# A new order for one core's 111 large transfers and the work between them, in a kernel with a branch near its end

## The chip, the cores and the metric

The kernel runs on one core of a Trainium2 chip. The metric is the device time of one execution in microseconds (us): 263.57 us is the median of three runs before the change (263.34 to 264.36).

## The reference

Four batches of 12,544 queries, keys and values of width 128, with 49 agent vectors per batch. Agents attend to keys and values, queries attend to agents, and a three-way maxout feed-forward network of width 768 follows.

```python
def sm(a, b):
    s = scale * (a @ b.transpose(0, 2, 1))
    s = s - s.max(-1, keepdims=True)
    e = np.exp(s)
    return e / (e.sum(-1, keepdims=True) + 1e-09)
agent_v = sm(agents, k) @ v
x = (sm(q, agents) @ agent_v).reshape(B * S, D)
h = np.maximum(np.maximum(x @ w1, x @ w2), x @ w3)
return (h @ w_out).astype(np.float32)
```

Inputs and output are float32 and live in HBM: some 78.7 MB are read and 25.7 MB written.

## The kernel before

**Keys and values.** Each batch is cut into 14 chunks of 896 rows; two chunks come in one load of 896 KB (`kl`, `vl`, line 274 issues them). A chunk of keys is cast to bf16 on POOL (`kc`), transposed on PE (`kt`), copied out of PSUM by DVE (`ke`), scored against the agents on PE (`ks`) and exponentiated on ACT (`kx`). A chunk of values is cast (`vc`, on ACT for batch 0, on POOL after that), and PE accumulates the products (`kv`).

**The batch's matrices.** When the last chunk of batch b is in, DVE normalises (`nr`, lines 352 and 353), PE multiplies by differences of the weights (`pu`, `pv`), ACT and DVE find for each agent and hidden unit which of the three maxout branches wins (`vs`, `tm`, `rd`, lines 369 to 391), PE counts the units whose winner isn't the same for all agents (`ps`), DVE gives them slots (`sl`, lines 409 to 412), and PE, ACT and DVE fill a matrix G of the batch (`px`, `py`, `gx`, `gy`), with which the network's work on a query becomes small.

**Queries.** 49 groups of 1,024 queries, two to a load of 1,024 KB (`ql`, line 476), group 48 with a half load of its own. A group is cast on POOL (`qc`, line 488), transposed (`qt`) and copied out by ACT (`qe`, line 494), scored (`sc`), exponentiated (`ex`, line 507), summed (`su`, `re`), multiplied by G (`u`, `v`), passed through the maxout (`a` on ACT, `x` on DVE, line 530), multiplied out into two PSUM banks (`li`, `p`) and scaled by DVE into an output slot (`ov`, line 546). Two groups share an output slot and one store of 1,024 KB (`st`, line 481); the last three stores are of 512 KB.

**The branch.** After the fourth batch's `sl`, DVE reduces the slot counts to one number in `most` (`fullest`, lines 416 and 417). Every engine loads that number (line 244) and branches on it (line 245): over the limit of 64 the general path would run, else the `Else` block goes on with the rest of the order. With these inputs it is the `Else` block. Nothing behind the branch is issued on an engine before that engine has taken it.

**What sets the order.** All this is one list of names, `ORDER`, in which `|` is the branch and a number behind a slash the buffer slot that the step's new tile takes; the program is emitted in exactly that order, and each engine runs its own part of it in order. SP issues all loads and stores and nothing else. There are 10 load slots (`LD`), 7 output slots (`OS`), 8 PSUM banks (`M`) and a few bf16 buffers of each kind. A load waits until the casts from its slot's old tile are done, and a scaling into an output slot until the store from it has landed, seven stores back. Transfers carry one of eight completion semaphores in turn: in the built program every transfer from the eighth on waits for the one eight places before it, so that at most eight are under way.

## Time and profile before

| | us |
|---|---|
| median of three runs | 263.57 |
| the profiled execution | 263.26 |
| its span, first to last instruction | 261.5 |
| what lies around the span | 1.76 |
| PE busy | 204.4 |
| DVE busy | 163.7 |
| ACT busy | 143.8 |
| POOL busy | 146.4 |

A row of the page's second part cuts the span into 40 slices of 6.54 us; its digits are tenths, its GB/s what the core's 16 DMA queues moved. SP is never counted as busy: its rows in a timeline are the issues of transfers. "Landing" is the time from a transfer's issue to the last of its 16 parts.

### The profile page before, as it was taken

How to read it: one execution, taken by the hardware profiler on the slowest of the kernel's cores; microseconds unless marked ns; L12 is line 12 of the kernel's file. 1: busy time of each engine (PE TensorE's matmuls, PEld its weight loads, DVE VectorE, ACT ScalarE, POOL GpSimd, SP SyncE). 2: the span in 40 equal slices, each digit the busy share in tenths (PEclk: the TensorE clock that was granted, in tenths of full speed). 3: DMA queues.
4: the chain of work that ended last, by engine and by line, in shares of the span. 5: the costliest groups of instructions: out<-in, count | busy, mean ns of one | idle time of the engine just before them, and what ended most of it. 6: DMA issues, size and time to landing. Idle time of an engine off the chain costs nothing.

```text
span 261.5 us, 7474 instructions
## 1 busy us (share of the span) xinstructions
PE 204.4 (78%) x3049; PEld 159.5 (61%) x3049; DVE 163.7 (63%) x337; ACT 143.8 (55%) x236; POOL 146.4 (56%) x164
## 2 busy tenths in 40 slices
PE   0775868699999995999877798867889645999950
PEld 0654657478778774787765576654666434777730
DVE  5352314748678779696657886641667833788980
ACT  1453555356677772637745665615457641899710
POOL 2423355997888869576765775475845561354000
PEclk9995595779999999799999999977999995999996
DMA  7999999999999999999999999999999976999995
GB/s 259 412 404 410 420 417 414 420 418 418 418 420 422 414 420 418 427 416 418 422 427 417 424 426 420 423 422 419 427 420 422 418 305 231 373 421 421 415 427 222
DMA packets 17639, 105.01 MB, mean 402 GB/s; under 512 B 1783, under 2 KB 3771, under 8 KB 11579
## 3 DMA queue, kind: packets, MB, share of 16 engines
q1 hardware_dynamic: 17392, 104.34, 97.1%
q8 instruction: 26, 0.43, 0.7%
q14 instruction: 18, 0.15, 0.2%
q10 hardware_dynamic: 203, 0.10, 0.1%
HBM read 78.74 MB, written 25.69 MB: 399 GB/s over the span
## 4 chain that ended last, share of the span: by engine, by line
DMA 72%; PE 19%; issue 2%; ACT 2%; DVE 1%; POOL 1%; DVEq 0%; SPq 0%; POOLq 0%; ACTq 0%
DMA LD<-in_q_dram 28%; DMA LD<-in_v_dram 23%; DMA LD<-in_k_dram 15%; PE psum L258 14%; DMA LD<-in_moe_w_out_dram 5%; PE psum L289 4%; ACT QT L494 1%; POOL QB L488 1%; DVE OS L546 1%; POOL KB L284 0%; ACT EK L304 0%; DVE R L530 0%; DVE KT L295 0%; ACT EQ L507 0%; DVEq L741 0%
## 5 line engine op out<-in xcount | busy, mean ns | idle before, releaser
L488 POOL CAST QB<-LD 128x1024 bf16<-128x1024 f32 x49 | 50.2, 1048 | 44.7 <-DMA LD<-in_q_dram 25.0
L546 DVE TENSOR_TENSOR OS<-psum,RC 128x512 f32<-128x512 f32 x98 | 63.4, 684 | 18.1 <-PE psum L258 16.0
L284 POOL CAST KB<-LD 128x896 bf16<-128x896 f32 x56 | 51.8, 951 | 39.9 <-DMA LD<-in_k_dram 34.0
L494 ACT ACTIVATE QT<-psum 128x1024 bf16<-128x1024 bf16 x49 | 50.3, 1026 | 33.0 <-PE psum L289 31.0
L295 DVE COPY KT<-psum 128x896 bf16<-128x896 bf16 x56 | 34.0, 614 | 32.5 <-PE psum L289 32.0
L284 POOL CAST VB<-LD 128x896 bf16<-128x896 f32 x42 | 38.6, 946 | 5.5 <-DMA LD<-in_v_dram 4.8
L258 PE MATMUL psum<-G,EQ 128*128 128x256 bf16 x196 | 38.7, 279 | 1.5 <-issue 1.5
L507 ACT ACTIVATE EQ<-psum 128x512 bf16<-128x512 f32 x49 | 29.1, 601 | 18.8 <-PE psum L258 18.4
L289 PE MATMUL psum<-ident,KB 128*128 128x128 bf16 x392 | 34.5, 242 | 6.3 <-POOL KB L284 5.8
L258 PE MATMUL psum<-G,R 128*128 128x256 bf16 x196 | 38.7, 280 | 0.7 <-DVE R L530 0.7
L289 PE MATMUL psum<-ident,QB 128*128 128x128 bf16 x392 | 31.8, 227 | 8.9 <-POOL QB L488 4.5
L289 PEld LDWEIGHTS <-QB 128*128 128x128 bf16 x392 | 26.4, 102 | 17.4 <-POOL QB L488 6.5
L530 DVE TENSOR_TENSOR R<-psum,AS 128x512 bf16<-128x512 f32 x49 | 33.1, 677 | 6.3 <-ACT AS L527 4.8
L527 ACT ACTIVATE AS<-psum 128x512 bf16<-128x512 f32 x49 | 29.2, 601 | 14.0 <-PE psum L258 8.4
L289 PEld LDWEIGHTS <-KB 128*128 128x128 bf16 x392 | 27.7, 109 | 11.6 <-POOL KB L284 8.1
L258 PE MATMUL psum<-QT,agT 128*128 128x512 bf16 (+1 forms) x104 | 30.9, 386 | 4.9 <-ACT QT L494 4.6
L304 ACT ACTIVATE EK<-psum 128x343 bf16<-128x343 f32 x56 | 24.7, 459 | 15.5 <-PE psum L258 14.4
L258 PEld LDWEIGHTS <-EQ 128*128 128x128 bf16 x392 | 26.8, 98 | 10.2 <-ACT EQ L507 2.8
L258 PE MATMUL psum<-EQ,G 128*128 128x512 bf16 (+1 forms) x104 | 31.8, 373 | 0.0
L258 PEld LDWEIGHTS <-ones 128*128 128x128 bf16 x417 | 19.1, 100 | 14.4 <-issue 11.8
L258 PE MATMUL psum<-EK,ones 128*128 128x49 bf16 x392 | 20.1, 190 | 5.9 <-ACT EK L304 5.9
L258 PEld LDWEIGHTS <-KT 128*128 128x128 bf16 x392 | 16.5, 102 | 9.6 <-DVE KT L295 6.2
(81 smaller groups left out, 201.5 us busy)
## 6 DMA issues: line engine op xcount, KB each, us to landing
LD<-in_k_dram SPq DMA_DIRECT2D x28, 896.0 KB, 18.2
LD<-in_v_dram SPq DMA_DIRECT2D x28, 896.0 KB, 18.1
LD<-in_q_dram SPq DMA_DIRECT2D x24, 1024.0 KB, 18.3
out_dram<-OS SPq DMA_DIRECT2D x23, 1024.0 KB, 18.5
out_dram<-OS SPq DMA_DIRECT2D x3, 512.0 KB, 6.8
LD<-in_moe_w_dram SPq DMA_DIRECT2D x3, 384.0 KB, 11.1
LD<-in_q_dram SPq DMA_DIRECT2D x1, 512.0 KB, 17.8
LD<-in_moe_w_out_dram SPq DMA_DIRECT2D x1, 384.0 KB, 14.1
```

The source lines that it names most:

```text
L258: self.nc.tensor.matmul(out, w, x, start=start, stop=True, skip_group_check=True)
L284: self.nc.gpsimd.tensor_copy(out=out, in_=src)
L289: self.nc.tensor.transpose(t[:, j * P:(j + 1) * P], src[:, j, :], self.ident)
L295: return lambda: self.nc.vector.tensor_copy(out=self.t[f"kT{r}"], in_=self.t[f"kT_ps{r}"].bitcast(BF16)[:, :KT * C])
L304: return lambda: self.nc.scalar.activation(self.t[f"e{r}"], self.t[f"s{r}"][:, :KT * A], AF.Exp, scale=SCALE)
L488: return lambda: self.nc.gpsimd.tensor_copy(out=self.t[f"qb.{s}"], in_=self.half("q", s))
L494: return lambda: self.nc.scalar.activation(self.t[f"qT.{s}"].rearrange("p j c -> p (j c)"), self.t[f"qT_ps.{s}"].bitcast(BF16), AF.Copy)
L507: return lambda: self.nc.scalar.activation(self.t[f"e.{s}"], self.t[f"qs.{s}"], AF.Exp, scale=SCALE)
L527: return lambda: self.nc.scalar.activation(self.t[f"a.{s}"], self.t[f"u.{s}"], AF.Relu)
L530: return lambda: self.nc.vector.tensor_tensor(out=self.t[f"r.{s}"], in0=self.t[f"v.{s}"], in1=self.t[f"a.{s}"], op=ALU.max)
L546: self.nc.vector.tensor_tensor(out=out[:, 4 * o:4 * o + 4, :], in0=src.rearrange("p (j c) -> p j c", c=C), in1=rc[:, 4 * o:4 * o + 4].unsq ...
```

## The change

Only the table `ORDER` is replaced: the same names in another order, with other slots. On SP the first eight transfers stay. Two of the weights' loads (`lw3`, `lwo`) come three transfers later. The first query load is the 19th transfer (was the 21st) and the later ones come up to four transfers sooner; the first store is the 53rd transfer (was the 47th). Ahead of `|` stand now two query loads more (`ql.40`, `ql.42`) and the same 13 stores. Of the diff, the line of the table with the branch:

```diff
-su.35 u.35/0 fullest v.35/5 st.25 px3/2 re.34/4 x.34/1 a.35/2 sc.36/6 re.35/5 gx3 x.35/2 qc.48/2 py3/7 ex.36/1 | qt.37/3 ql.40/9
+gx3 sc.37/3 x.34/1 qc.39/1 | ex.37/2 qt.48/6 gy3 li.34.0/1 qe.48/2 qc.40/2 su.37 p.34.0 x.35/2 li.34.1/7 p.34.1 ql.44/1 st.27
```

SP between the last value load (`vl3.12`) and the branch, before; `LD` are load slots, `OS` output slots, the 256-wide load is group 48's:

```order
L481 DMA out_dram<-OS_114 128x2048
L476 DMA LD_69<-in_q_dram 128x2048
L481 DMA out_dram<-OS_115 128x2048
L476 DMA LD_72<-in_q_dram 128x2048
L481 DMA out_dram<-OS_116 128x2048
L476 DMA LD_70<-in_q_dram 128x4x256
L476 DMA LD_73<-in_q_dram 128x2048
L481 DMA out_dram<-OS_117 128x2048
L244 TENSOR_LOAD most
L245 COMPARE_AND_BRANCH
```

And now, from the same place:

```order
L476 DMA LD_72<-in_q_dram 128x2048
L481 DMA out_dram<-OS_113 128x2048
L476 DMA LD_73<-in_q_dram 128x2048
L481 DMA out_dram<-OS_114 128x2048
L476 DMA LD_74<-in_q_dram 128x4x256
L476 DMA LD_69<-in_q_dram 128x2048
L481 DMA out_dram<-OS_115 128x2048
L476 DMA LD_65<-in_q_dram 128x2048
L481 DMA out_dram<-OS_116 128x2048
L476 DMA LD_70<-in_q_dram 128x2048
L481 DMA out_dram<-OS_117 128x2048
L244 TENSOR_LOAD most
```

Eight transfers stood between the last value load and the branch, now eleven: one store and two query loads more. The value load itself has one store fewer ahead of it. Behind the branch two query loads are left (were four) and the same 13 stores.

DVE from the fourth batch's `nr` to its `tm`, before; `kr` and `avT` are `nr`, `R_103` is `x.33`, `cand` is `tm`:

```order
L352 RECIPROCAL kr<-psum 128x49
L353 TENSOR_TENSOR avT_144<-psum,kr 128x49
L530 TENSOR_TENSOR R_103<-psum,AS_100 128x512
L380 SCALAR_TENSOR_TENSOR cand<-psum,cand 128x294
L381 TENSOR_TENSOR cand<-cand,psum 128x294
```

And now; the rows into `OS_113` scale groups 30 and 31, and the reciprocal is group 34's:

```order
L352 RECIPROCAL kr<-psum 128x49
L353 TENSOR_TENSOR avT_144<-psum,kr 128x49
L546 TENSOR_TENSOR OS_113<-psum,RC_106 128x512 x2
L546 TENSOR_TENSOR OS_113<-psum,RC_107 128x512 x2
L517 RECIPROCAL RC_110<-psum 128x8
L380 SCALAR_TENSOR_TENSOR cand<-psum,cand 128x294
```

One maxout step stood between them, now four scalings and a reciprocal. The scalings write the slot `OS_113`, so they wait until `st.17`, the store from it that stands second in the SP piece above, has landed.

DVE from the end of `rd` to `most`, before:

```order
L391 TENSOR_SCALAR open<-shut 128x6
L546 TENSOR_TENSOR OS_114<-psum,RC_109 128x512 x2
L409 SCALAR_TENSOR_TENSOR slot<-psum,open 128x6
L410 TENSOR_TENSOR pick<-slot_of,slot 128x384
L412 COPY counts<-psum 128x1
L416 TENSOR_REDUCE gap<-counts 128x1
L417 CAST most<-gap 128x1
```

And now:

```order
L391 TENSOR_SCALAR open<-shut 128x6
L517 RECIPROCAL RC_111<-psum 128x8
L546 TENSOR_TENSOR OS_114<-psum,RC_108 128x512 x2
L409 SCALAR_TENSOR_TENSOR slot<-psum,open 128x6
L410 TENSOR_TENSOR pick<-slot_of,slot 128x384
L412 COPY counts<-psum 128x1
L517 RECIPROCAL RC_106<-psum 128x8
L416 TENSOR_REDUCE gap<-counts 128x1
L417 CAST most<-gap 128x1
```

Two reciprocals came in; the scalings between are group 32's into `OS_114` (were group 33's). Group 33's stand now behind `most`. On PE, the transposes and scores of group 37 have moved from behind the branch to ahead of it; the products of groups 34 and 35 with G are ahead of it in both.

## The prediction

> **What bounds the kernel now.** I read the page's slices first, then windows around the one place where they drop, then the issues of SP there, then DVE and PE on both sides of it.

> ```profile
> DMA  7999999999999999999999999999999976999995
> GB/s 259 412 404 410 420 417 414 420 418 418 418 420 422 414 420 418 427 416 418 422 427 417 424 426 420 423 422 419 427 420 422 418 305 231 373 421 421 415 427 222
> ```
> ```profile
> 6.50:211.00 204.50, 169.50 (x2691) 133.87 (x2692) 129.99 (x260) 116.30 (x195) 133.08 (x145) 0.91 1.02 419
> 211.00:219.00 8.00, 3.54 (x41) 2.29 (x41) 1.79 (x4) 2.61 (x6) 3.35 (x4) 0.84 0.53 181
> 219.00:257.50 38.50, 31.32 (x317) 23.30 (x317) 28.28 (x56) 23.57 (x36) 8.20 (x9) 0.94 1.01 410
> 257.50:261.50 4.00, 0.00 (x0) 0.00 (x0) 0.00 (x0) 0.00 (x0) 0.00 (x0) 0.50 0.25 100
> ```

> The last two figures of a window are the DMA queues' share and GB/s. From 6.5 to 211 us the queues are full (1.02) at 419 GB/s, so transfers bound that stretch whatever the engines do. At 211 the flow breaks for eight microseconds. The finer windows show how:

> ```profile
> 211.00:214.00 3.00, 1.44 (x28) 0.86 (x28) 0.69 (x1) 1.58 (x5) 1.30 (x2) 1.00 0.80 321
> 214.00:217.00 3.00, 0.18 (x2) 0.18 (x3) 0.00 (x0) 0.00 (x0) 1.04 (x1) 0.91 0.29 104
> 217.00:219.00 2.00, 1.92 (x13) 1.25 (x11) 1.10 (x3) 1.02 (x1) 1.01 (x1) 0.50 0.47 86
> 219.00:222.00 3.00, 1.57 (x8) 1.14 (x9) 1.13 (x2) 0.00 (x0) 0.03 (x1) 0.50 0.97 399
> 222.00:229.00 7.00, 7.00 (x81) 5.49 (x80) 4.90 (x10) 5.54 (x8) 2.29 (x3) 0.91 1.00 371
> ```

> The share falls over six microseconds, not at once: the 16 queues run dry one after another, the first at about 211, the last at about 217. Against 419 GB/s the loss is 8 x (419-181) + 3 x (419-399) + 7 x (419-371) = 2,300 KB, 5.5 us in the mean over the queues. The cause stands in SP's issues (start, length) and its waits:

> ```profile
> 177.71 0.33 SPq L274 DMA_DIRECT2D LD<-in_k_dram  x1
> ...
> 182.06 0.34 SPq L481 DMA_DIRECT2D out_dram<-OS  x1
> ...
> 186.69 0.34 SPq L481 DMA_DIRECT2D out_dram<-OS  x1
> ...
> 198.36 1.75 SPq L481 DMA_DIRECT2D out_dram<-OS  x1
> 217.25 0.34 SPq L476 DMA_DIRECT2D LD<-in_q_dram  x1
> ```
> ```profile
> SPq L244 <- DVE RC L517: 10.2, 1, 10.2
> ...
> SPq L741 <- SPq L741: 6.2, 1, 6.2
> ```
> ```profile
> out_dram<-OS SPq DMA_DIRECT2D x1, 1024.0 KB, 18.8
> ```
> ```profile
> LD<-in_q_dram SPq DMA_DIRECT2D x1, 1024.0 KB, 5.2
> ```

> SP issues nothing for 18.9 us: 10.2 us it waits for the branch's number, then 6.2 us pass in the jump. The last store before the stop (198.36) lands 18.8 us later, at 217.2; the first load behind it (217.25) lands after 5.2 us, at 222.4, of which 1,049 KB at 419 GB/s are 2.5. So the last queue stood still from 217.2 to about 219.9, 2.7 us, and the first for some 8.

> [...]

> Behind the stop two bounds lie close together:

> ```profile
> 216.80:229.00 12.20, 10.67 (x100) 8.06 (x101) 7.13 (x14) 6.56 (x9) 3.33 (x4) 0.73 0.89 325
> 229.00:250.00 21.00, 21.00 (x220) 15.39 (x217) 18.54 (x38) 17.72 (x28) 5.88 (x6) 1.00 1.02 421
> ```
> ```profile
> 251.24 2.47 DVE L546 TENSOR_TENSOR OS<-psum,RC 128x512 f32<-128x512 f32 x4
> ```
> ```profile
> out_dram<-OS SPq DMA_DIRECT2D x1, 512.0 KB, 6.8
> ```

> From 229 to 250 PE is busy all 21.00 us while the queues are full as well (1.02). DVE's last scaling ends at 253.71; the last store, issued at once, still takes 6.8 us behind earlier ones and lands at 260.5, 1.0 us before the span's end.

> **The change, part by part.** Bytes and instructions are the same, and in the full stretch a transfer's time follows from the bytes ahead of it.

> *SP before the stop.* Two query loads more stand ahead of the branch: 2 x 1.049 MB at 419 GB/s are 5.0 us, so SP's last issue moves from 198.4 to 203.4. That holds if the queues stay full until then. The first store now comes six places later, so the bf16 buffers and load slots are refilled in a longer stretch of loads alone; each load still reuses a slot at least nine or ten places old, as before, and the eight transfers under way (18 us) cover a late cast of a few microseconds. I take 0 for it; without that cover, each microsecond of an empty queue is one of time. The two weights' loads that moved by three places are needed by the first batch's matrices much later: 0.

> *The number for the branch.* In the 85th place, where the last value load now stands, a load was issued at 177.71; with the median landing below it is in at 195.8. The rows of today's chain:

> ```profile
> LD<-in_v_dram SPq DMA_DIRECT2D x28, 896.0 KB, 18.1
> ...
> out_dram<-OS SPq DMA_DIRECT2D x23, 1024.0 KB, 18.5
> ```
> ```profile
> 198.35 1.82 POOL L284 CAST VB<-LD 128x896 bf16<-128x896 f32 x2 [0.34 <-DMA LD<-in_v_dram]
> ```
> ```profile
> 201.09 1.29 DVE L546 TENSOR_TENSOR OS<-psum,RC 128x512 f32<-128x512 f32 x2 [0.18 <-PE psum L258]
> 202.68 0.47 DVE L352 RECIPROCAL kr<-psum 128x49 f32<-128x49 f32 x1 [0.30 <-PE psum L258]
> ...
> 204.62 0.47 DVE L380 SCALAR_TENSOR_TENSOR cand<-psum,cand 128x294 f32<-128x294 f32 x1 [0.63 <-ACT cand L369]
> ...
> 207.71 0.17 DVE L391 TENSOR_SCALAR open<-shut 128x6 bf16<-128x6 f32 x1
> ...
> 208.99 0.15 DVE L409 SCALAR_TENSOR_TENSOR slot<-psum,open 128x6 f32<-128x6 f32 x1
> ...
> 210.03 0.15 DVE L417 CAST most<-gap 128x1 int32<-128x1 f32 x1
> ```

> From the casts' start to `kr` takes 4.3 us now; that puts `nr` at 200.2 and its end at about 200.9. Now four scalings follow on DVE. They need the slot of `st.17`, in the 87th place, where a store was issued at 182.06; at 18.5 us it lands at 200.6, so that wait is just covered. Four scalings (1.29 for two) 2.6 and a reciprocal 0.2: 203.7. From `cand` to the end of `open` is 3.3 today: 207.0. Then a reciprocal and two scalings, 1.5 (their slot is free when the 89th transfer lands, 186.69 + 18.5 = 205.2): 208.5. From `slot` to the cast's end 1.2, and one reciprocal more: 209.9, against 210.18. So the value load's 2.5 us are spent again on DVE, and the number comes when it came.

> *The stop.* 7.1 us lie between the cast's end and SP's next issue (210.18 to 217.25): SP issues again at 217.0. Its silence shrinks from 18.9 to 13.6 us. The first queue ran dry 12.6 us after the last issue and the last one 18.8 after: now 216.0 and 222.2. New data moves about 2.7 us after the issue, at 219.7. The last queues lose nothing; those that dry up before 219.7 (3.7 of 6.2 us, some 6 in 10) lose 1.9 on average, 1.1 in the mean over all. The gain on the DMA side is 2.7 for the last queue, and 5.5 - 1.1 = 4.4 in the mean. Which counts depends on whether the queue that is late at the stop is also the late one at the end: the last landing goes from 260.5 to 256.1 to 257.8.

> *Engines behind the stop.* They resume about when they did:

> ```profile
> 216.82 1.03 PE L289 MATMUL psum<-ident,QB 128*128 128x128 bf16 x8 [4.26 <-issue]
> ```
> ```profile
> L289 PE MATMUL psum<-ident,QB 128*128 128x128 bf16 x392 | 31.8, 227 | 8.9 <-POOL QB L488 4.5 <-issue 4.3
> ...
> L258 PE MATMUL psum<-QT,agT 128*128 128x512 bf16 (+1 forms) x104 | 30.9, 386 | 4.9 <-ACT QT L494 4.6
> ```

> PE has one group's transposes (31.8/49 = 0.65) and scores (30.9/49 = 0.63) less behind the branch, 1.3 us of an engine that is busy throughout; DVE has one maxout step more and one reciprocal less. So the last scaling ends between 252.4 and 253.7. With the queues less behind, the last half-size store takes about 5.2 - 1.25 = 3.9 instead of 6.8: landing at 256.3 to 257.6.

> *Sum.* Both bounds end within 256.1 to 257.8; the later of the two is taken, 257.2. With 1.0 to the span's end and the 1.76 around the span this is 260.0, against the profiled 263.26; the median of the runs shown, 263.57, lies 0.3 higher, and I leave the forecast at **260.0**. Its own range is 258.5 to 261.5: both bounds at their ends, and a microsecond or so for an order behind the branch that no row shows.

> **The rivals.** About 0.5% (1.3 us) is what a measurement of this kernel can tell from no change: below 262.25 is faster, above 264.9 slower.

> *The tail on the engines is no shorter.* PE and DVE are both nearly full from 229 on, and the order of 15 groups there is new. If the last scaling comes 2 to 3.5 us later than 253.7, the time is 262 to 263.9. For: 21.00 of 21.00. Against: PE has 1.3 us less to do. Chance 0.09.

> *The jump takes longer, because code is now fetched through full queues.* In the old stop the share was 0.80, then 0.29, while the code came in.

> ```profile
> DMA packets 17639, 105.01 MB, mean 402 GB/s; under 512 B 1783, under 2 KB 3771, under 8 KB 11579
> ...
> q8 instruction: 26, 0.43, 0.7%
> ```

> A fetch of this kind occupied a queue for 1.1 us (0.7% of 16 x 261.5 us, over 26), in traffic mostly full; how long one stands in line isn't shown. [...] Chance 0.10. [...]

> *Slower: the branch's number comes late.* Place: DVE behind `nr`, where the four scalings now stand ahead of `cand` and wait for the landing of `st.17`; 200.6 against 200.9 leaves 0.3 us. Each microsecond by which that slot, or the one for group 32, is late delays `most`, the jump on all five engines, and the full tail alike. From 2.3 us late the gain is under 0.5%; from 4.9 on the kernel is slower by more than that; at 5.5 it takes 265.5. Against it: landings of 18.1 to 18.8 in steady flow. Chance 0.13.

> *Better than forecast:* the new tail leaves PE and DVE fewer gaps, and both bounds sit at the low end: 257 to 258.5. Chance 0.08.

> That the change doesn't do what it says is no rival: the built order has the eleven transfers ahead of the branch.

> **How the numbers follow.** Forecast 0.60. Faster: 0.60 + 0.08, and 0.03 of the first two rivals' lower ends, 0.71. Same: the rest of those two, 0.16. Slower: 0.13. The range 258.0 to 263.6 leaves out the slower case (0.13), the lower half of the better one (0.04) and the top of the longer jump (0.03).

> **What would show it.** Right: SP's last store before the stop near 203.4, the first load behind it near 217, a silence of 13 to 14 us; the share above 0.8 in every window there; the last landing 3 to 5 us after the last scaling, not 6.8. Wrong: `most` later than 212 with DVE waiting for a store's landing in front of a scaling; a jump clearly over 6.2 us on SP; a share under 1 anywhere between 45 and 200 us, which would mean that the longer stretch of loads alone outran the casts; or a last scaling later than 255.

## The result and the profile after

The changed kernel takes 259.82 us (median of 4 runs, 259.46 to 260.06), the kernel before 263.73 on the same chip (4 runs, 263.34 to 264.36): ratio 0.9849, 95% interval 0.9825 to 0.9872. The profiled execution took 259.46 us, its span 257.6.

The page's slices, and windows of which the last two figures are the queues' share and GB/s:

```profile
DMA  7999999999999999999999999999999999999977
GB/s 256 411 419 408 399 424 414 419 419 417 415 420 422 414 417 421 416 417 423 423 421 422 424 421 426 421 419 421 420 422 422 421 425 359 382 425 417 423 328 307
```
```profile
6.50:211.00 204.50, 169.90 (x2697) 133.14 (x2715) 129.97 (x260) 119.50 (x197) 135.54 (x148) 0.91 1.02 419
211.00:219.00 8.00, 2.53 (x37) 1.68 (x31) 2.29 (x6) 0.64 (x3) 0.87 (x2) 0.83 0.97 371
219.00:245.00 26.00, 24.45 (x251) 18.30 (x255) 20.47 (x40) 20.85 (x32) 8.28 (x8) 0.92 1.01 411
245.00:252.00 7.00, 5.76 (x51) 3.94 (x50) 6.84 (x14) 3.27 (x6) 0.00 (x0) 1.00 0.80 330
```

The long stretch of loads keeps its 419 GB/s, so nothing was lost there. The hole at 211 to 219 is nearly filled (share 0.97, it was 0.53). A new dip stands at the end: 330 GB/s from 245 to 252, where SP has nothing to issue until DVE has scaled (it waits 4.2 us at the longest). SP's issues around the stop, and its waits:

```profile
203.34 0.34 SPq L481 DMA_DIRECT2D out_dram<-OS  x1
216.80 0.34 SPq L476 DMA_DIRECT2D LD<-in_q_dram  x1
```
```profile
SPq L244 <- DVE most L417: 6.8, 1, 6.8
SPq L741 <- SPq L741: 5.5, 1, 5.5
```

The silence is 13.5 us (it was 18.9). DVE's chain to the number, its last scalings, PE's and ACT's first rows behind the stop, and PE's last wait:

```profile
198.83 0.47 DVE L352 RECIPROCAL kr<-psum 128x49 f32<-128x49 f32 x1 [1.62 <-PE psum L258]
...
200.86 2.48 DVE L546 TENSOR_TENSOR OS<-psum,RC 128x512 f32<-128x512 f32 x4 [1.32 <-DMA out_dram<-OS]
204.58 0.21 DVE L517 RECIPROCAL RC<-psum 128x8 f32<-128x8 f32 x1 [1.24 <-PE psum L258]
...
210.30 0.15 DVE L417 CAST most<-gap 128x1 int32<-128x1 f32 x1
```
```profile
251.31 2.47 DVE L546 TENSOR_TENSOR OS<-psum,RC 128x512 f32<-128x512 f32 x4
```
```profile
217.71 1.01 PE L289 MATMUL psum<-ident,QB 128*128 128x128 bf16 x8 [5.47 <-issue]
...
219.67 0.27 PE L258 MATMUL psum<-sel,EQ 128*128 128x2 bf16 x4 [0.52 <-ACT EQ L507]
...
250.85 0.39 PE L258 MATMUL psum<-G,R 128*128 128x256 bf16 x2 [1.19 <-DVE R L530]
```
```profile
219.02 0.60 ACT L507 ACTIVATE EQ<-psum 128x512 bf16<-128x512 f32 x1 [7.37 <-DVE G L456]
```
```profile
out_dram<-OS SPq DMA_DIRECT2D x3, 512.0 KB, 2.9
```

The last scaling ends at 253.78, where it ended before (253.71). What is gained is its store: 2.9 us instead of 6.8. So the end now follows the engines, and that they weren't later than before has a reason of its own, which the experiments bring out.

### The profile page after: what moved, and what is told of

Same layout as the page of the kernel before. It is cut to its first block, busy times and chain, and to the rows that moved or that the text cites. A ratio compares the mean times of both kernels' runs of the same rounds, so it can differ in the third digit from the quotient of the medians.

```text
span 257.6 us, 7440 instructions
## 1 busy us (share of the span) xinstructions
PE 203.2 (79%) x3028; PEld 157.3 (61%) x3049; DVE 164.9 (64%) x337; ACT 145.5 (56%) x236; POOL 146.2 (57%) x164
## 2 busy tenths in 40 slices
DMA packets 17637, 104.99 MB, mean 407 GB/s; under 512 B 1783, under 2 KB 3771, under 8 KB 11579
## 4 chain that ended last, share of the span: by engine, by line
DMA 76%; PE 11%; issue 4%; DVE 4%; ACT 2%; POOL 0%; DVEq 0%; SPq 0%; ACTq 0%
DMA LD<-in_q_dram 43%; DMA LD<-in_v_dram 25%; PE psum L258 9%; DMA LD<-in_k_dram 7%; PE psum L289 3%; DMA ag_st<-in_agents_dram 2%; DVE OS L546 2%; ACT QT L494 1%; DVE R L530 1%; ACT EQ L507 0%; DVE gap L388 0%; POOL QB L488 0%; DVE RC L517 0%; DVEq L741 0%; ACT AS L527 0%
## 5 line engine op out<-in xcount | busy, mean ns | idle before, releaser
L488 POOL CAST QB<-LD 128x1024 bf16<-128x1024 f32 x49 | 50.3, 1048 | 42.3 <-DMA LD<-in_q_dram 19.7
L284 POOL CAST KB<-LD 128x896 bf16<-128x896 f32 x56 | 51.5, 948 | 38.5 <-DMA LD<-in_k_dram 23.9
L546 DVE TENSOR_TENSOR OS<-psum,RC 128x512 f32<-128x512 f32 x98 | 63.0, 678 | 15.4 <-DMA out_dram<-OS 8.3
L494 ACT ACTIVATE QT<-psum 128x1024 bf16<-128x1024 bf16 x49 | 50.1, 1023 | 20.5 <-PE psum L289 20.1
L284 POOL CAST VB<-LD 128x896 bf16<-128x896 f32 x42 | 38.3, 940 | 6.2 <-DMA LD<-in_v_dram 6.2
L258 PE MATMUL psum<-G,EQ 128*128 128x256 bf16 x196 | 39.0, 282 | 1.4 <-DVE OS L546 1.2
L289 PE MATMUL psum<-ident,QB 128*128 128x128 bf16 x392 | 31.8, 227 | 10.3 <-issue 5.5
L258 PE MATMUL psum<-G,R 128*128 128x256 bf16 x196 | 38.9, 281 | 1.2 <-DVE R L530 1.2
L289 PE MATMUL psum<-ident,KB 128*128 128x128 bf16 x392 | 34.5, 238 | 6.0 <-POOL KB L284 4.1
L289 PEld LDWEIGHTS <-QB 128*128 128x128 bf16 x392 | 25.9, 102 | 18.9 <-issue 7.9
L304 ACT ACTIVATE EK<-psum 128x343 bf16<-128x343 f32 x56 | 25.3, 458 | 21.5 <-PE psum L258 20.7
L527 ACT ACTIVATE AS<-psum 128x512 bf16<-128x512 f32 x49 | 28.8, 598 | 14.7 <-PE psum L258 12.7
L289 PEld LDWEIGHTS <-KB 128*128 128x128 bf16 x392 | 26.8, 106 | 14.2 <-POOL KB L284 10.0
L258 PE MATMUL psum<-QT,agT 128*128 128x512 bf16 (+1 forms) x104 | 30.5, 383 | 5.7 <-ACT QT L494 5.5
L258 PEld LDWEIGHTS <-EQ 128*128 128x128 bf16 x392 | 26.3, 99 | 10.5 <-ACT EQ L507 3.0
L258 PEld LDWEIGHTS <-ones 128*128 128x128 bf16 x417 | 18.7, 100 | 12.5 <-issue 8.2
L258 PE MATMUL psum<-EQ,G 128*128 128x512 bf16 (+1 forms) x83 | 24.8, 366 | 1.0 <-issue 0.2
L258 PE MATMUL psum<-EK,ones 128*128 128x49 bf16 x392 | 20.4, 191 | 5.2 <-ACT EK L304 5.1
L258 PE MATMUL psum<-agT,KT 128*128 128x49 bf16 x392 | 20.7, 192 | 4.6 <-DVE KT L295 4.1
## 6 DMA issues: line engine op xcount, KB each, us to landing
LD<-in_k_dram SPq DMA_DIRECT2D x28, 896.0 KB, 18.2
LD<-in_v_dram SPq DMA_DIRECT2D x28, 896.0 KB, 18.2
LD<-in_q_dram SPq DMA_DIRECT2D x24, 1024.0 KB, 18.4
out_dram<-OS SPq DMA_DIRECT2D x23, 1024.0 KB, 18.3
out_dram<-OS SPq DMA_DIRECT2D x3, 512.0 KB, 2.9
LD<-in_q_dram SPq DMA_DIRECT2D x1, 512.0 KB, 17.9
```

What stands on the lines that cost most here:

```text
L258: self.nc.tensor.matmul(out, w, x, start=start, stop=True, skip_group_check=True)
L284: self.nc.gpsimd.tensor_copy(out=out, in_=src)
L289: self.nc.tensor.transpose(t[:, j * P:(j + 1) * P], src[:, j, :], self.ident)
L304: return lambda: self.nc.scalar.activation(self.t[f"e{r}"], self.t[f"s{r}"][:, :KT * A], AF.Exp, scale=SCALE)
L488: return lambda: self.nc.gpsimd.tensor_copy(out=self.t[f"qb.{s}"], in_=self.half("q", s))
L494: return lambda: self.nc.scalar.activation(self.t[f"qT.{s}"].rearrange("p j c -> p (j c)"), self.t[f"qT_ps.{s}"].bitcast(BF16), AF.Copy)
```

## The experiments

Each median stands beside its ratio to the kernel before, measured in the same set of runs on the same chip, since that kernel's own median went from 263.7 to 264.4 from one set to the next (263.9 and 264.4 on one and the same chip).

### The two query loads alone

My first theory: the two loads ahead of the branch bring the gain, and behind the stop the engines set the end. `two_ahead` gives only these loads to the order of before.

```
- ... ex.36/1 | qt.37/3 ql.40/9 ... x.36/0 ql.42/0 qe.38/0
+ ... ex.36/1 ql.40/9 ql.42/0 | qt.37/3 ... x.36/0 qe.38/0
```

> The order of before, with nothing changed but the query loads for groups 40 and 42, which now stand ahead of the branch. Theory (these two loads bring the gain): SP's last issue ahead of the branch moves from 198.4 to about 203.4, its silence falls from 18.9 to about 14 us, the last scaling stays near 253.7 and the last store lands 3 to 4 us behind it: 259.6 to 260.6 us. Rival (the new order of everything else brings it, the longer stretch of loads and the new tail): no more than 0.5 us off 263.7.

264.35 us, ratio 1.0019 (0.9989 to 1.0049): no gain. SP's silence fell to some 12 us, and yet the last scaling ended at 257.84 instead of 253.71:

```profile
200.87 3.60 SPq L476 DMA_DIRECT2D LD<-in_q_dram  x2
216.30 1.44 SPq L481 DMA_DIRECT2D out_dram<-OS  x2
```
```profile
255.37 2.47 DVE L546 TENSOR_TENSOR OS<-psum,RC 128x512 f32<-128x512 f32 x4
```

PE's rows behind the branch in this run, and the last of them as it stands in the kernel before, at the same product:

```profile
218.56 1.03 PE L289 MATMUL psum<-ident,QB 128*128 128x128 bf16 x8 [5.94 <-issue]
219.39 0.63 PE L258 MATMUL psum<-G,EQ 128*128 128x256 bf16 x2
219.82 0.63 PE L258 MATMUL psum<-G,R 128*128 128x256 bf16 x2
220.25 0.42 PE L258 MATMUL psum<-G,EQ 128*128 128x256 bf16 x1
224.57 0.39 PE L258 MATMUL psum<-G,EQ 128*128 128x256 bf16 x1 [3.91 <-issue]
```
```profile
220.43 0.40 PE L258 MATMUL psum<-G,EQ 128*128 128x256 bf16 x1 [1.51 <-issue]
```

PE stops twice: in the jump (5.94 us, before 4.26), and again after 13 products (8 + 2 + 2 + 1, each with its weight load, so 26 instructions), waiting for nothing that the profile shows, for 3.91 us where before had 1.51. Together 1.7 + 2.4 = 4.1, all of the lateness. The second stop is in the middle of one group's work, and the profile names nothing that PE waits for, so it is hardly data. The new theory: it is code, which comes in blocks. The path that runs begins 26 instructions ahead of the end of a block; the next block comes late, by 1.51 us in the kernel before and by 3.91 here, where the queues are full of loads. In the changed kernel 28 instructions (14 products) more stand ahead of the branch on PE, so that by this theory its path begins 2 instructions behind that end and has a whole block ahead of it.

```profile
q8 instruction: 1, 0.02, 6.2%
```

Narrow windows give its time, 221.85 to 223.21; PE goes on 1.4 us after its end. In the kernel before, the packet lies at 217.50 to 219.16 and PE goes on 1.3 us later. So it is at the jump as well: a packet at 216.06 to 217.10 in `two_ahead` and at 214.34 to 215.38 in the kernel before, each ended 1.4 to 1.5 us before PE's first product. The next block's fetch began 0.7 us after PE's return in the kernel before, where the queues had run dry (share 0.47 from 217 to 219), and 3.3 us after it in `two_ahead`, where they were full (1.04 from 219 to 222).

### The two loads put back, the number made late, the tail made light

`two_behind` is the changed order with the two loads behind the branch.

```
- ql.40/0 ov.31.0 ... ps3/7 ql.42/5 qc.48/2 ... qc.39/1 | ex.37/2
+ ov.31.0 ... ps3/7 qc.48/2 ... qc.39/1 | ql.40/0 ql.42/5 ex.37/2
```

> The changed order, with the same two loads put back right behind the branch. Theory (these two loads bring the gain): SP's silence is back at 18 to 19 us, the queues run dry before the first load behind the stop moves, the last store lands 6 to 7 us behind the last scaling: 262.5 to 263.8 us. Rival (the rest of the new order brings it): 259.5 to 260.3.

262.54 us, ratio 0.9950 (0.9929 to 0.9972). The engines end at 250.84, 3 us sooner than in the changed kernel (PE is back 1.5 us sooner, at 216.19), and the last stores land 8.8 us behind:

```profile
248.36 2.48 DVE L546 TENSOR_TENSOR OS<-psum,RC 128x512 f32<-128x512 f32 x4
```
```profile
out_dram<-OS SPq DMA_DIRECT2D x3, 512.0 KB, 8.8
```

The queues set this end. The loads are needed in the new order, too; the half per cent that is left without them is hardly more than what the place of the code gives by itself, below.

`light_tail` takes work from the engines; it leaves out the hidden layer of the last groups, so its output is another:

```
+        if name.split(".")[0] in ("u", "v", "a", "x", "p") and int(name.split(".")[1]) >= 36:
+            return
```

> The changed kernel without the hidden layer (both shifted products, the relu, the maximum and the second output product) of groups 36 to 48; loads, softmax, linear part, scaling and stores stay. Theory (the tail is set by PE and DVE, not by the queues): the stores of the tail come sooner, the queues stay full to the end, 1.0 to 2.4 us less: 257.4 to 258.8. Rival (the queues set the end anyway): no more than 0.5 us less, 259.3 to 259.9.

259.04 us, ratio 0.9823 (0.9784 to 0.9861): the bound that the queues set in the changed order, 0.8 us under the changed kernel, between the two ranges. The last scaling ends at 245.83 + 4.28 = 250.11, the last store 6.2 us later, at 256.3.

```profile
245.83 4.28 DVE L548 TENSOR_TENSOR OS<-psum,RC 128x512 f32<-128x512 f32 x7
```
```profile
out_dram<-OS SPq DMA_DIRECT2D x3, 512.0 KB, 6.2
```

Against `two_behind` (250.84 + 8.8 = 259.6) the two loads are worth 3.3 us to the queues.

`late_number` holds the number back (`waste` is set up once, at the start):

```
     def fullest(self):
+        for _ in range(8):
+            self.nc.vector.tensor_tensor(out=self.waste, in0=self.waste, in1=self.waste, op=ALU.max)
```

> The changed kernel, with eight more maxima of a 256-wide tile that nothing uses, on DVE right ahead of the branch's number, about 2.5 us. Theory (behind the stop the engines set the end, and the number sets when they start): the last scaling moves by the whole 2.5 us, 262.0 to 262.6. Rival (the queues set the end; they hold work for 18 us behind SP's last issue, and a silence of 16 us stays hidden in most of them): no more than 0.8 us longer, 260.6 at most.

263.05 us, ratio 0.9986 (0.9959 to 1.0013), outside both ranges, and no clean test: the eight operations took 5.0 us, twice what I planned, so that SP's silence (18.4 us) was nearly that of before and the queues ran dry again (share 0.56 from 221.7 to 223.7).

```profile
209.59 5.01 DVE L419 TENSOR_TENSOR waste<-waste 128x256 f32<-128x256 f32 x8
```
```profile
203.42 0.34 SPq L485 DMA_DIRECT2D out_dram<-OS  x1
221.85 0.34 SPq L480 DMA_DIRECT2D LD<-in_q_dram  x1
```

What it shows is the price of the slower rival: a number 4.4 us late (214.86 against 210.45) costs 3.2 us by the medians, 3.6 by the ratios, 0.7 to 0.8 us for each.

### Where the branch's target lies in PE's program

The general path stands between the branch and the path that runs. Products that are added to it never run; they only move the target.

```
     def in_general(self):
         nc, ps, slots = self.nc, self.psum, self.slots
+        for _ in range(16):
+            self.mul(ps[:, 7, :64], self.ones, self.earlier[:, :64], True)
```

`two_ahead_page` is `two_ahead` with 16 such products, 32 instructions:

> The order of before with the two query loads ahead of the branch, and 16 products more in the general path, which is never taken: they run in no execution and only move PE's straight path 32 instructions further back in its program. Theory (the two loads alone lost because PE, 26 instructions behind the branch's target, ran out of fetched code a second time, 3.9 us there against 1.5 in before): the second idle stretch is gone, the last scaling comes at about 254, 259.6 to 261.0 us. Rival (the old order's tail is too slow with loads this early): 263.5 to 265.

259.69 us, ratio 0.9828 (0.9793 to 0.9863), against 264.35 without the dead code. PE stops only once, and runs on over the place where it had stopped; the last scaling is at 253.80:

```profile
218.18 1.03 PE L289 MATMUL psum<-ident,QB 128*128 128x128 bf16 x8 [5.85 <-issue]
219.01 0.63 PE L258 MATMUL psum<-G,EQ 128*128 128x256 bf16 x2
219.44 0.63 PE L258 MATMUL psum<-G,R 128*128 128x256 bf16 x2
219.86 0.63 PE L258 MATMUL psum<-G,EQ 128*128 128x256 bf16 x2
```

`after_page` is the changed kernel with 114 such products. Its target lies 28 + 2 x 114 = 256 instructions behind that of the kernel before; with blocks of that length, the 256 to a packet counted above, it is 26 ahead of an end again:

> The changed kernel with 114 products more in the general path, which is never taken, so that PE's straight path again begins 26 instructions ahead of the place where before ran out of code. Theory (where the branch's target lies in PE's program decides): a second idle stretch of 3 to 4 us on PE some 26 instructions behind the branch, the last scaling at 256 to 258, 262.3 to 264.0 us. Rival (it doesn't matter): 259.4 to 260.3.

261.84 us, ratio 0.9902 (0.9866 to 0.9939): 2.0 us slower than the changed kernel by the medians, 1.4 by the ratios, whose intervals just touch, and half a microsecond under the range expected. The trace is plainer: the stop is there, after 13 products as in before (8 + 2 + 3), 2.57 us where 3 to 4 were expected, with a fetch at 219.38 to 220.35, and the last scaling ends at 256.32:

```profile
219.10 0.24 PE L258 MATMUL psum<-sel,EQ 128*128 128x2 bf16 x3 [1.05 <-ACT EQ L507]
221.91 0.16 PE L258 MATMUL psum<-sel,EQ 128*128 128x2 bf16 x1 [2.57 <-issue]
```
```profile
253.84 2.48 DVE L546 TENSOR_TENSOR OS<-psum,RC 128x512 f32<-128x512 f32 x4
```

`before_page` is the kernel before with 16:

> The kernel before with 16 products more in the general path, which is never taken. Both theories of the code's place take PE's second idle stretch of 1.5 us away. If the queues set the end of before (the two loads bring the gain): no more than 0.4 us off 263.7, the last scaling near 252.2 and the last store 8 us behind it. If the engines did (the code's place alone brings it): 262.0 to 262.4.

263.37 us, ratio 0.9963 (0.9929 to 0.9996), from runs between 261.61 and 265.04. The second stop is gone and the last scaling ends at 253.13, 0.6 us sooner where 1.5 were expected, but the last stores take 8.3 us: the queues set the end of before, so PE's 1.5 us bought at most a little.

```profile
out_dram<-OS SPq DMA_DIRECT2D x3, 512.0 KB, 8.3
```

So in the order of before the two edits make a square, neither worth much without the other:

| order of before | target 26 ahead of a block's end | target at a block's start |
|---|---|---|
| two loads behind the branch | 1 (the kernel before) | 0.9963 |
| two loads ahead | 1.0019 | 0.9828 |

In the new order three corners were measured: 0.9950 (behind, at a start), 0.9902 (ahead, at an end) and 0.9849 (ahead, at a start: the change).

### A sooner number and a sooner branch

`early_branch` moves the maximum, test and positions of the last batch up on DVE, and the branch up on every engine:

```
- ... ex.34/4 ql.40/0 ov.31.0 ... ov.31.1 ... tm3 ... rd3 ... ps3/7 ... sl3 ... fullest ... qc.39/1 |
+ ... ex.34/4 ql.40/0 tm3 rd3 ov.31.0 ... ps3/2 ov.31.1 sl3 fullest ... st.23 ql.42/5 st.25 ... sc.36/3 |
```

> The changed order with the last batch's maximum, test and positions ahead of the scalings of group 31 on DVE, so that the branch's number comes 2 to 3 us sooner, and the branch right behind the scores of group 36, with the same transfers ahead of it. Theory (the changed kernel's end is set by the engines, 0.8 us above what its queues would allow): resumption at 213.5 to 215, SP silent for 10 to 12 us, queues never dry, 258.0 to 259.3 us. Rival (DVE's order costs as much as the earlier jump saves): 259.5 to 261.

262.79 us, ratio 0.9936 (0.9895 to 0.9978), outside both ranges. The number came 2.3 us sooner and SP issued again at 214.41, but PE's last products ahead of the branch ended at 211.68 (212.24 in the changed kernel), and it now had 66 products more to do behind it, counted in the built order:

```profile
207.96 0.15 DVE L417 CAST most<-gap 128x1 int32<-128x1 f32 x1
```
```profile
205.87 0.17 PE L258 MATMUL psum<-open,earlier 128*128 128x7 bf16 x1 [1.45 <-DVE open L391]
...
211.09 0.59 PE L258 MATMUL psum<-QT,agT 128*128 128x512 bf16 x2 [0.36 <-ACT QT L494]
217.81 1.01 PE L289 MATMUL psum<-ident,QB 128*128 128x128 bf16 x8 [6.13 <-ACT EQ L507]
...
223.21 0.58 PE L258 MATMUL psum<-QT,agT 128*128 128x512 bf16 x1 [0.72 <-issue]
```

PE lost 1.45 us waiting for `open` in the middle of its work. Half a microsecond was left of the 2.3, and the jump took 0.7 more: the ACT step that its row names had ended 0.9 us before, PE's fetch of code 1.6 us before. Both executions compared here had a PE clock of 0.50 from 200 to 206 (two 256-wide products took 0.63 us at 203.3). Against `after_page`, at 1.00 there (0.38 us at 205.1), the number came 1.2 us sooner and PE reached the branch 0.9 us later. The last scaling ended at 257.44.

PE also stopped a second time, for 0.72 us, in the last row above. The branch stands 132 instructions (66 products) sooner on PE than in the changed kernel, so that its target has 132 - 2 = 130 instructions to the block's end. The stop comes after 65 products, just there, and a fetch of code ended 1.35 us before PE went on (at 221.86).

### The jump taken away

Exchanging the two ways puts the path that runs right behind the branch, so that it isn't jumped to.

```
-        with self.tc.If(count > CAPACITY) as over:
-            self.in_general()
-        with over.Else():
+        with self.tc.If(count <= CAPACITY) as fits:
             for name in order[cut + 1:]:
                 self.emit(plan, name)
+        with fits.Else():
+            self.in_general()
```

> The changed kernel with the two ways of the branch exchanged: the test is written the other way round, the path that runs stands right behind the branch and the general path, never taken, behind it; the jump over the general path now comes at the end. Theory (the jump's 5.5 to 6 us on PE and SP are the wait for code at a far place): PE stands for 1 to 2 us at the branch, SP's silence is about 8 us, the last scaling comes at 248.5 to 250.5, and the queues set the end, 258.0 to 259.0 us. Rival (the jump is only moved to the end and paid there in full): 260 to 262.

259.06 us (258.88 to 259.29), ratio 0.9806 (0.9781 to 0.9831): just above the range, and by its median the fastest kernel that keeps the branch; its runs all lie under those of the changed kernel, though the two intervals touch. SP's silence is 7.0 us, PE doesn't stop, and its clock in the window of the old stop is 1.00 (it was 0.83):

```profile
203.50 0.34 SPq L481 DMA_DIRECT2D out_dram<-OS  x1
210.48 0.33 SPq L476 DMA_DIRECT2D LD<-in_q_dram  x1
```
```profile
210.17 0.61 PE L258 MATMUL psum<-QT,agT 128*128 128x512 bf16 x2
210.62 0.61 PE L289 MATMUL psum<-ident,QB 128*128 128x128 bf16 x8
```
```profile
211.00:219.00 8.00, 7.41 (x89) 5.64 (x88) 6.52 (x16) 6.47 (x10) 2.88 (x3) 1.00 1.01 422
```
```profile
out_dram<-OS SPq DMA_DIRECT2D x3, 512.0 KB, 10.3
```

The engines are done at 245.86, sooner than I had worked out (248.5 to 250.5), and the last stores land 10.3 us behind: only the queues are left, and a jump at the end lies beside their landing: the span ends 1.0 us behind it, as in the kernel before. I hadn't counted the clock, whose figure is the third from the right in a window. This one is of the changed kernel, behind its stop:

```profile
219.00:222.00 3.00, 2.26 (x14) 1.41 (x15) 2.08 (x4) 1.81 (x3) 0.99 (x1) 0.50 1.04 371
```

There two 256-wide products take 0.63 us, in `straight_first` 0.38. So the stop cost PE more than the time in which it stood.

`no_branch` emits the whole order in one piece:

```
-        cut = order.index("|")
-        for name in order[:cut]:
-            self.emit(plan, name)
...
+        for name in order:
+            if name != "|":
+                self.emit(plan, name)
```

> The changed order in one piece: the load of the number, the comparison and the general path are left out. Theory (behind a stop that is gone only the queues are left to bound the kernel): share full to the last stores, 257.3 to 258.6 us. Rival (the tail on PE and DVE sets the end even without a stop): the last scaling later than 250 and 258.8 to 259.8.

258.26 us, ratio 0.9777 (0.9752 to 0.9802). The last scaling ends at 245.96, far ahead of the rival's 250, so this is what the queues allow; the stop still costs the changed kernel 1.6 us by the medians, 1.9 by the ratios, and `straight_first` 0.8.

`before_straight` is the same exchange in the kernel before:

> The kernel before, its order untouched, with the two ways of the branch exchanged as in the run above. Theory (the two loads are worth what the stop's length makes them worth: the queues hold 12.6 to 18.8 us of work behind SP's last issue): a silence of about 13 us, only the first queues dry for a microsecond or two, 258.6 to 260.3 us. Rival (without the two loads ahead the queues break whatever the jump takes): 261 to 262.5.

259.27 us, ratio 0.9810 (0.9785 to 0.9835), as fast as `straight_first` within the intervals, with nothing in the order changed:

```profile
198.32 1.74 SPq L481 DMA_DIRECT2D out_dram<-OS  x1
211.06 0.33 SPq L476 DMA_DIRECT2D LD<-in_q_dram  x1
```

A silence of 12.7 us is about what the queues cover (share 0.98 from 211 to 219), so loads moved ahead of the branch have little left to bring. The new order is worth its 1.5% against the jump, and hardly anything without it.

## Why the prediction was right, and where not

- *SP.* Last issue 203.4, next one 217.0, silence 13.6: measured 203.34, 216.80, 13.5. Right.
- *The early stretch at 0.* Right: 419 GB/s and 1.02, as before.
- *The number.* Forecast 209.9, measured 210.45. The way there differed: `kr` came at 198.83, not 200.2, and the 1.4 us were lost waiting 1.32 us for the store's landing (200.84), the place that the slower rival named; then a reciprocal waited 1.24 for PE. That second wait belongs to the profiled execution: PE's granted clock was 0.50 from 200 to 206 in it. In `after_page` and `straight_first`, whose order up to the branch is the same, the clock there was 1.00, the wait was gone, and the number came at 209.27; what lowers the clock no run shows. `late_number` priced the rival: 4.4 us late gives 263.05, where a whole microsecond for each, as the prediction has it, would give 264.2. So that rival was there, but its price was too high by a fifth to a quarter.
- *The gain on the queues, 2.7 to 4.4.* Two kernels whose end the queues set give 3.3 (`two_behind` 259.6, `light_tail` 256.3). Right.
- *"Engines behind the stop. They resume about when they did", with 1.3 us less on PE, the last scaling at 252.4 to 253.7.* This step failed, although its number nearly held (253.78). PE resumed 0.9 us later: its work ahead of the branch ended 0.3 us sooner (212.24, before 212.56), but its jump grew from 4.26 to 5.47 us, which is the rival of the longer jump, in part; SP's shrank from 6.2 to 5.5. By how much code fetched through full queues lengthens a jump, no trace of before showed; measured were these 1.2 us on PE, and 1.7 to 1.8 from the two loads alone. ACT came back later still (219.02), and PE waited for it. All of PE's saving was spent, and what made up for it was nowhere in the prediction: the second stop, 1.51 us at 220.43 in the trace of before, fell away because the branch had moved by 28 instructions on PE. With that stop put back, the same change gives 261.84, just under the 262 to 263.9 of the rival of a tail that is no shorter, and the last scaling ends 2.6 us later than before, which is inside that rival's 2 to 3.5. I had quoted PE's row at 216.82 and not read the four rows behind it.
- *The last store, 3.9 us behind the last scaling.* Measured 2.9: SP had issued little ahead of it (330 GB/s from 245 to 252). Right in kind, a microsecond too long, and just outside the 3 to 5 us that were to show it.
- *Sum.* 260.0 against 259.82. The mechanism on the queues was right. For the engines the number came out by luck: an effect that the prediction didn't have made up for the longer jump on PE, which its sum left at nothing.

Right behind the branch PE stood 1.5 to 3.9 us for its second stop with 26 instructions to the block's end and 0.7 us with 130. The fetches are seen in the traces, the block's ends are not: where they lie is inferred from the 256 instructions to a packet, from what dead code did to the stop in three kernels, and from the product at which `early_branch` stopped.

PE's stop in the jump is 4.1 and 4.3 us in the two kernels whose queues were running dry when it jumped (before, `before_page`) and 5.5 to 5.9 in `two_ahead`, `two_ahead_page`, `two_behind`, `after_page` and the changed kernel. Two pairs differ by the two loads alone and jump at about the same moment: in before and `two_ahead` PE's last product ends at 212.56 and 212.63, and the stops are 4.26 and 5.94 us; in `before_page` and `two_ahead_page` it ends at 212.66 and 212.33, and they are 4.08 and 5.85. So the two loads make PE's jump 1.7 to 1.8 us longer. All of that lies ahead of the fetch, whose packet starts 1.8 us after PE's last product in before and 3.4 in `two_ahead`; from the packet's start to PE's first product it is 2.5 us in both. What the fetch waits for in that time no view shows.

## What to carry to other kernels

The jump of this branch cost a fetch of code at its target (PE stood 4.1 to 6.1 us) and, with the target 26 or 130 instructions ahead of a block's end, a second one that PE stood for (1.5 to 3.9 us, and 0.7): read the engine's rows behind a branch and the fetches beside them, and lay out the program so that the common path falls through (5 us here). Two limits that lie close together must be moved together: here the loads alone gave 1.0019, the code's place alone 0.9963, both 0.9828. And when an order is changed, ask what else moved with it, since the position of the code is part of the result.

## What the runs showed of the hardware that was not expected

- Code that never runs changed the time by 4.7 us (264.35 to 259.69) in one kernel and by 2.0 us the other way in another (medians; by the ratios 5.0 and 1.4).
- With 26 instructions to the block's end, PE's second stop was 1.51 us where the queues had run dry just before (share 0.47 from 217 to 219), 2.57 and 3.91 us where they had stayed nearly full (eight and nine tenths in the page's slice at 217). Behind the stops whose packet is given above PE went on 1.3 to 1.6 us after the packet's end.
- In the changed kernel PE's granted clock was 0.83 over the stop's window (211 to 219) and 0.50 from 217, just ahead of PE's return, to 222; in `straight_first`, without a stop, it was 1.00 in both.
- Exchanging the branch's two ways took 5 us from the kernel before (259.27 against 264.42), more than all of the new order did.
